# Two units at a time from unit 8 on, in the spectral stage of a Fourier layer with a gated feed-forward part

## The chip, the cores and the metric

One core of one Trainium2 chip. The metric is the time of one execution in microseconds on the device, lower is better. The engines are named as the profile names them: PE (TensorE), DVE (VectorE), ACT (ScalarE), POOL (GpSimd) and SP, whose queue issues every DMA of this kernel.

## The reference

For x of 8 x 3136 x 256, a Fourier transform along the 3136 positions, a complex 256 x 256 mix with bias, a soft threshold at 0.01, the transform back, and then a feed-forward part with a convolution of width 3 and a gate:

```python
X = np.fft.rfft(x, axis=1)
Yr = Xr @ w_r - Xi @ w_i + b_r
Yi = Xr @ w_i + Xi @ w_r + b_i
Yr, Yi = [np.sign(Y) * np.maximum(np.abs(Y) - 0.01, 0) for Y in (Yr, Yi)]
y = np.fft.irfft(Yr + 1j * Yi, n=3136, axis=1)
h = np.maximum(y @ w_in, 0)                      # 1024 channels
out = (h * sigmoid(conv3(h, conv_w))) @ w_out
```

## The kernel before, in words

3136 is 49 x 64, so each transform is two stages of small matrix products with a twiddle table between them. The work of the first 467 us of the span is cut into 50 *units* (`items`, L470): six groups of four frequencies for each of eight batches, and one more unit for each half of the batches. A unit passes through these steps:

- *Stage one* is not per unit but per *piece* (64 pieces of x): four products of 49 x 64 on quarters of the PE array (`quads`, L333), copied out by ACT and DVE (L350, L351), and stored to DRAM by SP. A unit has one or two pieces beside it, as long as pieces last (through unit 40).
- *Stage two* (`stage2`, L384): the rows `a2` come back from DRAM, and eight full-width products fill two PSUM banks, one for each half t of the 256 features. The results must be split into a high and a low part for the mix. For each half ACT copies the imaginary part into d (L387) and casts the whole into fh (L388); DVE makes d, the difference of the two (L389), and fl, the rest that the cast leaves (L390).
- *The third, derived part* (`third`): ACT casts d into fh (L395), and POOL forms its rest in fl (L396).
- *Mix* (`mix`, L412): 36 products of 128 x 256 into three banks c = 2, 0, 1, where c = 2 is the derived part. Each product reads fh or fl as the stationary operand. DVE then adds bank 2 to the bias for both outputs (L415) and joins banks 0 and 1 (L417).
- *Shrink* (`shrink`): two relus on ACT (L428, L429) and their difference on POOL (L430).
- *Stage three* (`stage3_pe`, L440, L443): sixteen products on quarters of the array, into the double bank `psa`, of which there is one; ACT copies it out as z1 (L450) and SP stores it.

PSUM has eight banks: `psa` takes two, and all other products share a ring of six, in the order in which they are asked for.

The order is written out by hand: inside this part each engine takes its instructions in the order of the program. Turn `it` of the loop at L571 issues stage three of unit it-4, the pieces, stage two of unit it, shrink of unit it-2, the third part of unit it, and the mix of unit it-1. So a unit's split is made a whole turn before its mix.

Beside this, `later` (L287) makes the weights of the feed-forward part out of 64-bit numbers, in small DVE *steps*, three a unit from unit 8 to 43. Ten steps (L264 to L271, L279, L280) make one block; the ninth, L279, subtracts what a cast on ACT (L278) leaves, and waits for it. In the last units *stage four* of the first batch (`stage4`, L159) is placed between the others. The feed-forward part after the units (L655 to L701) is not touched.

Of the kernel before, what the change touches and what calls it, by code (L numbers as in the profile page):

```python
# [9 lines left out]
F32 = mybir.dt.float32  # L10
# [13 lines left out]
SP = 64  # L24
H = C // 2
LAM = 0.01
UG = 4
# [84 lines left out]
def spectral_ffn_kernel(ctx: ExitStack, tc: tile.TileContext, x, w_r, w_i, b_r, b_i,  # L112
# [61 lines left out]
    with ExitStack() as ab:  # L174
# [198 lines left out]
                nc.sync.dma_start(a2[0:C], sc0[b // BH].rearrange("b j d -> j b d"))  # L373
            return a2

        def stage2(g, a2):

            fh, fl = [wkf.tile([P, NT, 3, UG, SP], F32R, name=nm) for nm in ("fh", "fl")]
            d = wkf.tile([P, NT, UG, SP], F32, name="d", bufs=DB)
            for t in range(NT):  # L380
                ps = psx.tile([P, UG, 2, SP], F32, name="ps_s2", tag="bank")
                for k in range(UG):
                    kk, q = (K2, g * UG + k) if g < NG else (C, U)
                    nc.tensor.matmul(ps[:, k], a2[0:kk, k, t * P:(t + 1) * P], t2[0:kk, q, :],  # L384
                                     start=(k == 0), stop=(k == UG - 1), skip_group_check=True)
                psv = ps.rearrange("p k c m -> p c k m")
                nc.scalar.copy(d[:, t], psv[:, 1])  # L387
                nc.scalar.copy(fh[:, t, 0:2], psv)  # L388
                nc.vector.tensor_tensor(d[:, t], psv[:, 0], d[:, t], op=ALU.subtract)  # L389
                nc.vector.tensor_tensor(fl[:, t, 0:2], psv, fh[:, t, 0:2].bitcast(F32), op=ALU.subtract)  # L390
            return fh, fl, d

        def third(xs):
# [2 lines left out]
            nc.gpsimd.tensor_tensor(fl[:, :, 2], d, fh[:, :, 2].bitcast(F32), op=ALU.subtract)  # L396
            return fh, fl

        def mix(xs):


            fh, fl = xs
            ps = {c: psx.tile([K2, UG // 2, D], F32, name=f"ps_mx{c}", tag="bank") for c in (2, 0, 1)}
            for c in (2, 0, 1):
                q = (1, 2, 0)[c]
                for k in range(UG // 2):
                    mm = []
                    for t in range(NT):
                        a = [f[:, t, c, 2 * k:2 * k + 2, :] for f in (fh, fl)]
                        mm += [(a[0], wmix_hi[:, t, q, :]), (a[0], wmix_lo[:, t, q, :]), (a[1], wmix_hi[:, t, q, :])]  # L410
                    for n, (lt, rh) in enumerate(mm):
                        nc.tensor.matmul(ps[c][:, k, :], lt, rh, start=(n == 0), stop=(n == len(mm) - 1))  # L412
            v = wk.tile([K2, 2, UG // 2, D], F32, name="v")
            for c in range(2):
                nc.vector.tensor_tensor(v[:, c], ps[2], bias[:, c:c + 1, :].to_broadcast([K2, UG // 2, D]), op=ALU.add)  # L415
            for c in range(2):
                nc.vector.tensor_tensor(v[:, c], ps[c], v[:, c], op=ALU.add)  # L417
            return v

        def clip(v):  # L420
# [9 lines left out]
            nc.gpsimd.tensor_tensor(r, r, v, op=ALU.subtract)  # L430
            return r

        def stage3_pe(g, r):
            ps = psa.tile([P, 2, UG // 2, D], F32, name="ps_s3")
            for a in range(2):
                for k in range(UG // 2):
                    for h in range(2):
                        rows = slice(SP * h, SP * (h + 1))
                        if g < NG:
                            nc.tensor.matmul(ps[SP * a:SP * (a + 1), h, k, :], i1[rows, a, g * UG // 2 + k, :], r[rows, a, k, :],  # L440
                                             start=(k == 0), stop=(k == UG // 2 - 1), skip_group_check=True)
                        else:
                            nc.tensor.matmul(ps[0:SP, h, k, :], i1[rows, a, U // 2, :], r[rows, a, k, :],  # L443
                                             start=(a + k == 0), stop=(a + k == UG // 2), skip_group_check=True)
            return ps

        def stage3_out(b, g, ps):
            z1 = io.tile([P, 2, UG // 2, D], F32, name="z1", bufs=2)
            n = P if g < NG else SP
            nc.scalar.copy(z1[0:n], ps[0:n])  # L450
            if g < NG:
                z1 = z1.rearrange("p h k e -> p (h k) e")
                for c in range(2):
# [18 lines left out]
        LAG, WP0, LATE, NW, NF0, NF1 = 4, 8, 10, 7, 14, 3  # L472
        xs, vs, ss, a2s, xq, pair = {}, {}, {}, {}, {}, []
        p1 = nx = NX

# [8 lines left out]
        def next_s1(p):  # L484
            return stage1_pe(xq[p // 2][:, p % 2])
# [68 lines left out]
        Y0, Y1 = n_it - 6, n_it - 1  # L554
        jgs = iter(range(NPC))

        def one_by_one():
# [10 lines left out]
            stage4(jg, z2, y0, one_by_one)  # L568
            ask_z2()

        for it in range(n_it + LAG):  # L571
            drain = it >= n_it
            if it:
                fetch(1)
            if 2 < it + 2 < NG and it % 2 == 0:
                load_t2(it + 2)
            elif it == LATE:
                load_t2(NG)
                load_inv1(NG)
# [5 lines left out]
            if drain:  # L585
                last_stage()
            if it >= LAG:
                g3 = items[it - LAG]
                ps3 = stage3_pe(g3[1], ss.pop(it - LAG))
            n_s1 = min(2 if 0 < it < 5 else (1, 2, 1, 1, 2, 1)[(it - 5) % 6] if it else 0, n_pc - p1)  # L590
            ps1 = [next_s1(p1 + i) for i in range(n_s1)] if it > 1 else []
            if it >= LAG:
                stage3_out(*g3, ps3)
            if WP0 <= it < Y0:
                next(background, None)
            elif it == WP0 - 2:
                next(background)
            for ps in ps1:
                stage1_out(p1, ps)
                p1 += 1  # L600
            ask_a2(it + 1)
            if WP0 <= it < Y0:
                for _ in range(2):
                    next(background, None)
            if it < n_it:
                xs[it] = stage2(items[it][1], a2s.pop(it))
            if it == Y0:
# [6 lines left out]
            if it == n_it - 1:  # L614
                xs[it] = third(xs[it])
            if 0 <= it - 2 < n_it:
                ss[it - 2] = (clip if drain else shrink)(vs.pop(it - 2))
            if it < n_it - 1:
                xs[it] = third(xs[it])
            if Y0 < it < Y1:  # L620
                last_stage()
            if it == 1:
                for _ in range(n_s1):
                    stage1_out(p1, next_s1(p1))
                    p1 += 1
            if 0 <= it - 3 < NG:
                fill_inv1(it - 3)
            if 0 <= it - 1 < n_it:
                vs[it - 1] = mix(xs.pop(it - 1))
# [121 lines left out]
```

## Time and profile before

| what | value |
|---|---|
| median of 3 runs | 1677.89 us (1676.13 to 1679.12) |
| the profiled execution | 1675.06 us, span 1673.3 us |
| PE busy | 1660.5 us, 99% of the span |
| DVE, ACT, POOL busy | 1388.7, 1177.1, 192.3 us |
| last stage three of the units begins | 465.05 us |
| first product of the feed-forward part | 466.92 us |

The page gives busy times of the engines, the span in 40 slices, the chain of work that ended last, and the costliest groups of instructions. In the timeline a row reads: start in us, length in us, engine, line, operation, tiles written and read, shapes, count, and in brackets the idle time before it with what ended it. A row of waits reads: engine, tile and line that waited, what it waited for, us in total, times, longest. PEld is the loading of a stationary operand, which runs beside the products.

### The profile page before, as it was taken

Reading aid. Unit: us, or ns where it says so; the run is one execution under the profiler, and the core shown is the slowest. Engines: PE = TensorE matmul, PEld = TensorE weight load, DVE = VectorE, ACT = ScalarE, POOL = GpSimd, SP = SyncE. Lnnn points to the kernel's source line nnn. Section 1 sums busy time; section 2 is a strip of 40 time slices with the busy share of each in tenths; the row PEclk is TensorE's granted clock in tenths of the full one; section 3 lists DMA queues with packets and bytes.
Section 4 is the critical chain, followed back from the end, with each engine's and each line's share of the span. In section 5 each row is a group of like instructions: output and inputs, shape, how many; then the busy total and the mean of one; then the engine's idle time right before and its main releaser. Section 6 shows DMA issues by size and latency. Waiting matters only on the chain.

```text
span 1673.3 us, 30664 instructions
## 1 busy us (share of the span) xinstructions
PE 1660.5 (99%) x12618; PEld 1541.2 (92%) x12618; DVE 1388.7 (83%) x1728; ACT 1177.1 (70%) x1585; POOL 192.3 (11%) x114
## 2 busy tenths in 40 slices
PE   9899999999999999999999999999999999999998
PEld 5788888889999999999999999999999999999998
DVE  3578888877688888888888888888888888888887
ACT  3577777777677677777677776767777776776776
POOL 1444444445300000000000000000000000000000
PEclk9999999999999999999999999999999999999999
DMA  8999999886421111111110111111101111100001
GB/s 228 282 292 291 259 268 270 248 230 190 109 81 42 51 33 42 52 52 42 52 47 27 42 36 36 43 52 52 33 33 52 52 34 50 42 23 23 23 23 45
DMA packets 108297, 162.29 MB, mean 97 GB/s; under 512 B 10842, under 2 KB 87806, under 8 KB 108094
## 3 DMA queue, kind: packets, MB, share of 16 engines
q1 hardware_dynamic: 108158, 160.34, 32.4%
q8 instruction: 100, 1.64, 0.4%
q14 instruction: 39, 0.32, 0.1%
HBM read 83.24 MB, written 77.07 MB: 96 GB/s over the span
## 4 chain that ended last, share of the span: by engine, by line
PE 98%; DMA 1%; issue 0%; SPq 0%; ACT 0%; ACTq 0%
PE acc L690 33%; PE ps_h L655 33%; PE ps_mx L412 13%; PE ps_s L159 7%; PE ps_s L384 6%; PE ps_s L333 3%; PE ps_s L440 3%; DMA a<-sch 0%; DMA hx<-in_x_dram 0%; PE ps_idle L509 0%; PE ps_s L443 0%; DMA sch<-ha 0%; SPq L316 0%; ACT o L696 0%; SPq L347 0%
## 5 line engine op out<-in xcount | busy, mean ns | idle before, releaser
L690 PE MATMUL acc<-wout,gh 128*128 128x256 f32 x3136 | 567.4, 281 | 0.4 <-ACT gh L676 0.4
L671 DVE SCALAR_TENSOR_TENSOR c<-h,cw,c 128x896 f32<-128x896 f32 x448 | 513.2, 1147 | 65.0 <-ACT c L669 63.8
L655 PE MATMUL ps_h<-yh,win 128*128 128x450 f32 (+1 forms) x1792 | 546.5, 366 | 0.0
L690 PEld LDWEIGHTS acc<-wout,gh 128*128 128x128 f32 x3136 | 491.0, 188 | 6.1 <-ACT gh L676 0.6
L690 PE MATMUL acc<-wout,gl 128*128 128x256 f32 x1568 | 436.0, 280 | 0.0
L665 ACT ACTIVATE h<-ps_h 128x898 f32<-128x898 f32 (+1 forms) x224 | 207.2, 925 | 231.6 <-PE ps_h L655 231.4
L655 PEld LDWEIGHTS ps_h<-yh,win 128*128 128x128 f32 x1792 | 337.6, 188 | 26.0 <-issue 0.4
L655 PE MATMUL ps_h<-yl,win 128*128 128x450 f32 (+1 forms) x896 | 328.7, 367 | 0.0
L690 PEld LDWEIGHTS acc<-wout,gl 128*128 128x128 f32 x1568 | 293.1, 188 | 0.2
L673 DVE TENSOR_TENSOR c<-h,c 128x896 f32<-128x896 f32 x224 | 243.6, 1088 | 48.1 <-ACT c L672 47.0
L677 DVE TENSOR_TENSOR gl<-c,gh 128x896 fp32r<-128x896 f32 x224 | 243.2, 1088 | 35.4 <-ACT gh L676 31.4
L676 ACT CAST gh<-c 128x896 fp32r<-128x896 f32 x224 | 210.5, 945 | 81.2 <-DVE c L673 81.1
L672 ACT ACTIVATE c<-c 128x896 f32<-128x896 f32 x224 | 213.5, 953 | 23.8 <-DVE c L671 21.1
L655 PEld LDWEIGHTS ps_h<-yl,win 128*128 128x128 f32 x896 | 168.5, 188 | 10.1
L669 ACT ACTIVATE c<-h,cw 128x896 f32<-128x896 f32 x168 | 175.5, 1045 | 2.9 <-DVE gl L677 0.2
L412 PE MATMUL ps_mx<-wmix_hi,fh 128*128 128x256 f32 x600 | 172.2, 287 | 0.0
L412 PE MATMUL ps_mx<-wmix_lo,fh 128*128 128x256 f32 x600 | 167.6, 279 | 0.0
L412 PE MATMUL ps_mx<-wmix_hi,fl 128*128 128x256 f32 x600 | 167.1, 279 | 0.0
L430 POOL TENSOR_TENSOR r<-r,v 128x1024 f32<-128x1024 f32 x48 | 114.5, 2385 | 217.8 <-ACT v L429 200.2
L384 PEld LDWEIGHTS ps_s<-t,a 128*128 128x128 f32 (+1 forms) x800 | 94.7, 194 | 37.9 <-issue 23.0
L159 PEld LDWEIGHTS ps_s<-i,z 98*128 98x128 f32 x1024 | 122.5, 192 | 1.9 <-issue 0.8
L159 PE MATMUL ps_s<-i,z 98*128 98x98 f32 x1024 | 123.3, 273 | 0.0
(93 smaller groups left out, 1672.7 us busy)
## 6 DMA issues: line engine op xcount, KB each, us to landing
z<-sc SPq DMA_DIRECT2D x64, 392.0 KB
sc<-z SPq DMA_DIRECT2D x96, 256.0 KB
out_dram<-o SPq DMA_DIRECT2D x27, 896.0 KB
xr<-in_x_dram SPq DMA_DIRECT2D x112, 192.0 KB
sc<-a SPq DMA_DIRECT2D x56, 384.0 KB
a<-sc SPq DMA_DIRECT2D x42, 512.0 KB
hx<-in_x_dram SPq DMA_DIRECT2D x16, 192.0 KB
a<-sch SPq DMA_DIRECT2D x6, 512.0 KB
```

The costliest lines, as they stand in the source:

```text
L159: nc.tensor.matmul(to, z2[:, j, t * P:(t + 1) * P], i2[:, 0 if jg or j else 1, :], start=(j == 0), stop=(j == JG - 1), skip_group_check=True)
L384: nc.tensor.matmul(ps[:, k], a2[0:kk, k, t * P:(t + 1) * P], t2[0:kk, q, :], start=(k == 0), stop=(k == UG - 1), skip_group_check=True)
L412: nc.tensor.matmul(ps[c][:, k, :], lt, rh, start=(n == 0), stop=(n == len(mm) - 1))
L655: nc.tensor.matmul(dst, lt, rh, start=(i == 0), stop=(i == len(mm) - 1))
L665: nc.scalar.activation(hv, src, AF.Relu)
L669: nc.scalar.mul(cv, tap(0), cw[:, 0, f:f + 1])
L671: nc.vector.scalar_tensor_tensor(cv, tap(k), cw[:, k, f:f + 1], cv, op0=ALU.mult, op1=ALU.add)
L672: nc.scalar.activation(c, c, AF.Sigmoid)
L673: nc.vector.tensor_tensor(cv, tap(1), cv, op=ALU.mult)
L676: nc.scalar.copy(gh, c)
L677: nc.vector.tensor_tensor(gl, c, gh.bitcast(F32), op=ALU.subtract)
L690: nc.tensor.matmul(acc[m // 2][:, m % 2, :], lt[:, sl], rh[:, f, :], start=(f == 0 and n == 0 and m % 2 == 0), stop=(f == NF - 1 and n == ...
```

## The change

Units 0 to 7 keep their turns. From unit 8 on a turn takes two units, u and u+1. On PE it issues stage three of u-4, up to two pieces, stage three of u-3, the other pieces; then both second stages; then both mixes. Where no piece lies between the two stage threes, the second takes two banks of the ring and not `psa`. In a pair:

- the mix of u follows the second stages of u and u+1 directly. In before it followed the next unit's second stage, pieces and stage three;
- DVE makes d for both halves and then fl for both halves, where it made d, fl, d, fl;
- the mix takes the derived part last: banks 0, 1, 2, and the bias is added to banks 0 and 1, bank 2 joined after;
- the relus of u-1 and u stand after both second stages, around the mix of u;
- of six steps a pair, four stand around the pieces, one before the mix of u and one after the relus of u;
- x is asked for at the start of the turn and again behind the pieces; a2 of u+2 at the start and behind the pieces, a2 of u+3 behind the second stage of u.

The core of the diff:

```diff
-        def stage2(g, a2):
+        def stage2(g, a2, paired=False):
+            made = []
...
                 nc.scalar.copy(d[:, t], psv[:, 1])
                 nc.scalar.copy(fh[:, t, 0:2], psv)
-                nc.vector.tensor_tensor(d[:, t], psv[:, 0], d[:, t], op=ALU.subtract)
-                nc.vector.tensor_tensor(fl[:, t, 0:2], psv, fh[:, t, 0:2].bitcast(F32), op=ALU.subtract)
+                made.append((t, psv))
+                if t or not paired:
+                    for k, src in made:
+                        nc.vector.tensor_tensor(d[:, k], src[:, 0], d[:, k], op=ALU.subtract)
+                    for k, src in made:
+                        nc.vector.tensor_tensor(fl[:, k, 0:2], src, fh[:, k, 0:2].bitcast(F32), op=ALU.subtract)
+                    made = []
...
-        def mix(xs):
+        def mix(xs, paired=False):
...
-            for c in (2, 0, 1):
+            order = (0, 1, 2) if paired else (2, 0, 1)
+            for c in order:
...
+        for u in range(PAIR, n_it, 2):
+            busy = u < Y0
+            ask_a2(u + 2)
+            fetch(2)
...
+            z = s3(u - LAG)
+            out1 = pieces(min(n_s1, 2))
+            next(out1)
+            if busy:
+                steps(2)
+            stage3_out(*z)
+            next(out1, None)
+            if busy:
+                steps(1)
+            z = s3(u + 1 - LAG, not n_s1)
+            out1 = pieces(max(n_s1 - 2, 0))
+            next(out1)
+            stage3_out(*z)
+            next(out1, None)
+            if busy:
+                steps(1)
+            fetch(2)
+            ask_a2(u + 2)
...
+            for i in (u, u + 1):
+                xs[i] = third(stage2(items[i][1], a2s.pop(i), True))
+                if i == u:
+                    ask_a2(u + 3)
+                if u > Y0:
+                    last_stage()
...
+            ss[u - 1] = shrink(vs.pop(u - 1))
+            if busy:
+                steps(1)
+            vs[u] = mix(xs.pop(u), True)
+            ss[u] = shrink(vs.pop(u))
+            if busy:
+                steps(1)
+            vs[u + 1] = mix(xs.pop(u + 1), True)
+
+        for n in range(2):
+            z = s3(n_it - LAG + n)
+            last_stage()
+            stage3_out(*z)
+            if n == 0:
+                ss[n_it - 1] = clip(vs.pop(n_it - 1))
+            last_stage()
+        z = [s3(n_it - 2 + n, n) for n in range(2)]
+        for q in z:
+            stage3_out(*q)
```

On PE, in the turn of unit 12 before: stage three, two pieces, one second stage, and the mix of unit 11 (fh_1594, while the second stage at hand belongs to unit 12).

```order
L440 MATMUL ps_s3_1667<-r_1503,i1_465 64x256 x8
L333 MATMUL ps_s1_1676<-xr_1226,f1_118 64x512 x2
L333 MATMUL ps_s1_1677<-xr_1226,f1_118 64x512 x2
L333 MATMUL ps_s1_1682<-xr_1446,f1_118 64x512 x2
L333 MATMUL ps_s1_1683<-xr_1446,f1_118 64x512 x2
L384 MATMUL ps_s2_1706<-t2_122,a2_1559 128x128 x4
L384 MATMUL ps_s2_1715<-t2_122,a2_1559 128x128 x4
L412 MATMUL ps_mx2_1730<-wmix_hi_125,fh_1594 128x256
L412 MATMUL ps_mx2_1730<-wmix_lo_126,fh_1594 128x256
L412 MATMUL ps_mx2_1730<-wmix_hi_125,fl_1595 128x256
```

The same unit now, in the pair of units 12 and 13, from the pair's second stage three on: fh_1788 and fl_1789 are the split of ps_s2_1791 and ps_s2_1798, four rows above.

```order
L463 MATMUL ps_s3_1751<-r_1609,i1_465 64x256 x8
L333 MATMUL ps_s1_1760<-xr_1300,f1_118 64x512 x2
L333 MATMUL ps_s1_1761<-xr_1300,f1_118 64x512 x2
L385 MATMUL ps_s2_1791<-t2_122,a2_1559 128x128 x4
L385 MATMUL ps_s2_1798<-t2_122,a2_1559 128x128 x4
L385 MATMUL ps_s2_1816<-t2_122,a2_1584 128x128 x4
L385 MATMUL ps_s2_1823<-t2_122,a2_1584 128x128 x4
L419 MATMUL ps_mx0_1841<-wmix_hi_125,fh_1788 128x256
L419 MATMUL ps_mx0_1841<-wmix_lo_126,fh_1788 128x256
L419 MATMUL ps_mx0_1841<-wmix_hi_125,fl_1789 128x256
```

The mix has moved next to its own unit's second stage, with one other second stage between them; the third product reads fl.

On DVE before, one unit's split and the adds behind the mix (d and fl in turn for the two halves):

```order
L389 TENSOR_TENSOR d_2033<-ps_s2_2034,d_2033 128x256
L390 TENSOR_TENSOR fl_2032<-ps_s2_2034,fh_2031 128x512
L389 TENSOR_TENSOR d_2033<-ps_s2_2043,d_2033 128x256
L390 TENSOR_TENSOR fl_2032<-ps_s2_2043,fh_2031 128x512
L415 TENSOR_TENSOR v_2097<-ps_mx2_2058,bias_123 128x512 x2
L417 TENSOR_TENSOR v_2097<-ps_mx0_2059,v_2097 128x512
L417 TENSOR_TENSOR v_2097<-ps_mx1_2060,v_2097 128x512
```

And now, in the pair of units 18 and 19: the splits of both units, a step, then the adds of the first mix.

```order
L393 TENSOR_TENSOR d_2446<-ps_s2_2447,d_2446 128x256
L393 TENSOR_TENSOR d_2446<-ps_s2_2454,d_2446 128x256
L395 TENSOR_TENSOR fl_2445<-ps_s2_2447,fh_2444 128x512
L395 TENSOR_TENSOR fl_2445<-ps_s2_2454,fh_2444 128x512
L393 TENSOR_TENSOR d_2471<-ps_s2_2472,d_2471 128x256
L393 TENSOR_TENSOR d_2471<-ps_s2_2479,d_2471 128x256
L395 TENSOR_TENSOR fl_2470<-ps_s2_2472,fh_2469 128x512
L395 TENSOR_TENSOR fl_2470<-ps_s2_2479,fh_2469 128x512
L268 TENSOR_SCALAR win_m_2389<-win_bits_1972 128x512
L423 TENSOR_TENSOR v_2536<-ps_mx0_2497,bias_123 128x512
L423 TENSOR_TENSOR v_2536<-ps_mx1_2498,bias_123 128x512
```

The first fl now stands behind the second d.

On ACT now, in the pair of units 16 and 17: the third casts, the relus of unit 15 (v_2151), a weight cast, the relus of unit 16, and the copy of the next stage three.

```order
L401 CAST fh_2239<-d_2241 128x2x256
L447 ACTIVATE r_2262<-v_2151,small_86 128x1024
L448 ACTIVATE v_2151<-v_2151,small_86 128x1024
L278 CAST win_0_82<-win_m_1977 128x512
L447 ACTIVATE r_2312<-v_2307,small_86 128x1024
L448 ACTIVATE v_2307<-v_2307,small_86 128x1024
L477 COPY z1_2394<-ps_s3_2363 128x1024
```

Before, a cast of this kind stood between the copies:

```order
L450 COPY z1_1903<-ps_s3_1888 128x1024
L278 CAST win_0_82<-win_m_1589 128x512
L350 COPY a1_1909<-ps_s1_1897 128x2x256
L387 COPY d_1924<-ps_s2_1925 128x256
L388 CAST fh_1922<-ps_s2_1925 128x512
```

It has moved from the head of a unit's copies to a place behind two relus.

More of the change, by code (lines that the diff above doesn't have):

```diff
@@ L397, in third @@
             return fh, fl
-        def mix(xs):
+        def mix(xs, paired=False):
             fh, fl = xs
-            ps = {c: psx.tile([K2, UG // 2, D], F32, name=f"ps_mx{c}", tag="bank") for c in (2, 0, 1)}
-            for c in (2, 0, 1):
+            order = (0, 1, 2) if paired else (2, 0, 1)
+            ps = {c: psx.tile([K2, UG // 2, D], F32, name=f"ps_mx{c}", tag="bank") for c in order}
+            for c in order:
                 q = (1, 2, 0)[c]
@@ L413, in mix, with biased, joined @@
             v = wk.tile([K2, 2, UG // 2, D], F32, name="v")
[L414 to L417, printed above, removed]
+            def biased(c, src):
+                nc.vector.tensor_tensor(v[:, c], ps[src], bias[:, c:c + 1, :].to_broadcast([K2, UG // 2, D]), op=ALU.add)
+            def joined(c, src):
+                nc.vector.tensor_tensor(v[:, c], ps[src], v[:, c], op=ALU.add)
+            if paired:
+                for c in range(2):
+                    biased(c, c)
+                for c in range(2):
+                    joined(c, 2)
+            else:
+                for c in range(2):
+                    biased(c, 2)
+                for c in range(2):
+                    joined(c, c)
             return v
@@ L431, in shrink, with stage3_pe @@
             return r
-        def stage3_pe(g, r):
-            ps = psa.tile([P, 2, UG // 2, D], F32, name="ps_s3")
+        def stage3_pe(g, r, ring=False):
+            if ring:
+                ps = [psx.tile([P, UG // 2, D], F32, name="ps_s3", tag="bank") for _ in range(2)]
+            else:
+                both = psa.tile([P, 2, UG // 2, D], F32, name="ps_s3")
+                ps = [both[:, h] for h in range(2)]
             for a in range(2):
@@ L449, in stage3_out @@
             n = P if g < NG else SP
-            nc.scalar.copy(z1[0:n], ps[0:n])
+            if isinstance(ps, list):
+                for h in range(2):
+                    nc.scalar.copy(z1[0:n, h], ps[h][0:n])
+            else:
+                nc.scalar.copy(z1[0:n], ps[0:n])
             if g < NG:
@@ L553, in spectral_ffn_kernel @@
         background = later()
-        Y0, Y1 = n_it - 6, n_it - 1
+        Y0 = n_it - 6
         jgs = iter(range(NPC))
@@ L569, in last_stage, with steps, s3, pieces @@
             ask_z2()
-        for it in range(n_it + LAG):
-            drain = it >= n_it
+        def steps(n):
+            for _ in range(n):
+                next(background, None)
+        def s3(i, ring=False):
+            b, g = items[i]
+            return b, g, stage3_pe(g, ss.pop(i), ring)
+        def pieces(n):
+            nonlocal p1
+            todo = [next_s1(p1 + i) for i in range(n)]
+            yield
+            for ps in todo:
+                stage1_out(p1, ps)
+                p1 += 1
+        for it in range(PAIR):
             if it:
@@ L598, in spectral_ffn_kernel @@
-            for ps in ps1:
-                stage1_out(p1, ps)
-                p1 += 1
-            ask_a2(it + 1)
[L602 to L607, printed above, removed]
+                z = s3(it - LAG)
+            n_s1 = 2 if 0 < it < 5 else (1, 2, 1, 1, 2, 1)[(it - 5) % 6] if it else 0
+            if it > 1:
+                out1 = pieces(n_s1)
+                next(out1)
@@ L613, in spectral_ffn_kernel @@
                     ask_z2()
[L614 to L629, printed above, removed]
+            ss[u - 1] = shrink(vs.pop(u - 1))
[4 more added lines that the diff above has]
+            if busy:
+                steps(1)
+            vs[u + 1] = mix(xs.pop(u + 1), True)
+        for n in range(2):
+            z = s3(n_it - LAG + n)
+            last_stage()
+            stage3_out(*z)
+            if n == 0:
[4 more added lines that the diff above has]
+            stage3_out(*q)
         assert p1 == n_pc and not z2s and next(background, True)
```

48 lines of the change are left out of this document (30 added, 18 removed).

## The prediction, made before the changed kernel was run

> **What bounds the kernel now.** I read the page first, then the list of waits, the stretches, and the timeline of one unit. The page's busy times and its chain of waits:
>
> ```profile
> PE 1660.5 (99%) x12618; PEld 1541.2 (92%) x12618; DVE 1388.7 (83%) x1728; ACT 1177.1 (70%) x1585; POOL 192.3 (11%) x114
> PE 98%; DMA 1%; issue 0%; SPq 0%; ACT 0%; ACTq 0%
> ```
>
> The chain is TensorE almost from end to end. Its waits, longest and last, and one stretch of the unit stage:
>
> ```profile
> PE ps_s L333 <- issue: 5.0, 1, 5.0
> ...
> PE acc L690 <- ACT gh L676: 0.4, 1, 0.4
> ```
>
> ```profile
> 200.00:250.00 50.00, 50.00 (x471) 41.96 (x470) 43.44 (x74) 37.02 (x58) 22.88 (x12) 1.00 0.97 266
> ```
>
> The 5.0 us lie at 43 us, before the units that change. From there on TensorE waits for nobody, at clock 1.00, while VectorE works 43.44 of 50 us and ScalarE 37.02. So nothing is to be gained but TensorE's own handovers, and any wait that the new order brings is lost whole. The timeline of a unit with one piece, and the start of the next, which has two:
>
> ```profile
> 200.31 0.28 PE L412 MATMUL ps_mx<-wmix_lo,fh 128*128 128x256 f32 x1
> 200.43 0.27 PE L412 MATMUL ps_mx<-wmix_hi,fl 128*128 128x256 f32 x1
> 200.64 1.11 PE L440 MATMUL ps_s<-r,i 64*64 64x256 f32 x16
> 201.55 1.05 PE L333 MATMUL ps_s<-xr,f 49*64 49x512 f32 x8
> 201.83 1.01 ACT L450 COPY z<-ps_s 128x1024 f32<-128x1024 f32 x1 [1.68 <-PE ps_s L440]
> 202.53 2.05 PE L384 MATMUL ps_s<-t,a 128*128 128x128 f32 x16
> 204.05 0.59 ACT L388 CAST fh<-ps_s 128x512 fp32r<-128x512 f32 x1
> 204.34 0.37 PE L412 MATMUL ps_mx<-wmix_hi,fh 128*128 128x256 f32 x1
> 204.55 0.19 PEld L412 LDWEIGHTS ps_mx<-wmix_hi,fl 128*128 128x128 f32 x1
> 204.73 0.42 DVE L389 TENSOR_TENSOR d<-ps_s,d 128x256 f32<-128x256 f32 x1
> 204.89 0.59 ACT L388 CAST fh<-ps_s 128x512 fp32r<-128x512 f32 x1
> 204.90 0.19 PEld L412 LDWEIGHTS ps_mx<-wmix_hi,fl 128*128 128x128 f32 x1
> 205.07 0.68 DVE L390 TENSOR_TENSOR fl<-ps_s,fh 128x512 fp32r<-128x512 f32 x1
> 205.67 0.41 DVE L389 TENSOR_TENSOR d<-ps_s,d 128x256 f32<-128x256 f32 x1
> 208.76 1.11 PE L440 MATMUL ps_s<-r,i 64*64 64x256 f32 x16
> 209.68 1.91 PE L333 MATMUL ps_s<-xr,f 49*64 49x512 f32 x16
> 211.52 2.05 PE L384 MATMUL ps_s<-t,a 128*128 128x128 f32 x16
> ```
>
> Each group begins where the one before it hands over: 0.91 us stage three, 0.98 one piece (1.84 two), 1.81 second stage, 4.42 mix. In this order the mix at 204.34 reads the unit before, whose splits are long done. The unit whose second stage began at 202.53 is mixed a whole unit later. That distance is what the change gives up.
>
> **What the change saves.** *Mix to stage three.* Mix matmuls follow each other at 0.12 us (200.31, 200.43); the next stage three comes 0.21 after the last. So 0.09 is lost once a unit, now once a pair: 21 x 0.09 = 1.9 us. Both ends are nearly equal, since second stage to mix shows no such loss.
>
> *Pieces to second stage.* A second piece costs 1.84 - 0.98 = 0.86, so the handover from a piece to the second stage is 0.12. It is now paid once a pair. The new handover, piece to stage three, is in no trace. Another row:
>
> ```profile
> 377.62 1.11 PE L440 MATMUL ps_s<-r,i 64*64 64x256 f32 x16
> 378.66 2.05 PE L384 MATMUL ps_s<-t,a 128*128 128x128 f32 x16
> ```
>
> Stage three straight into the second stage takes 1.04 where stage three into a piece takes 0.91: full-width loads behind quarter tiles pay 0.13. Between quarter tiles it can cost nothing or up to the same 0.12. I take half: 21 x 0.06 = 1.3 us, ends 0 and 2.5. A loss beyond that is excluded, since no handover in the rows is dearer than 0.13.
>
> *The end.* The last stage-four group is followed by one stage three, then by the first matmul of the next part:
>
> ```profile
> 465.05 1.94 PE L443 MATMUL ps_s<-r,i 64*64 64x256 f32 x16
> 466.92 0.19 PEld L655 LDWEIGHTS ps_h<-yh,win 128*128 128x128 f32 x1 [0.39 <-issue]
> ```
>
> These 1.87 hold 1.04 of work and 0.83 of waiting for y. In the new order two stage threes stand there and cover it: 0.8, ends 0 and 0.8. Saved in all 4.0 us, between 1.9 and 5.2.
>
> **What it costs: the splits come too late.** Put the start of second stage u at 0. A second stage with other full-width matmuls behind it takes 1.89:
>
> ```profile
> 407.64 2.05 PE L384 MATMUL ps_s<-t,a 128*128 128x128 f32 x16
> 409.53 1.93 PE L159 MATMUL ps_s<-i,z 98*128 98x98 f32 x16
> ```
>
> So mix u would begin at 1.89 + 1.81 = 3.70. It loads fl of the first half 0.21 later (204.55 - 204.34) and of the second half 0.56 later (204.90): wanted at 3.91 and 4.26. The other side: the cast fh of the second half ends at 204.89 + 0.59 - 202.53 = 2.95. VectorE starts 0.09 after such a cast (204.64 to 204.73), and now does both d first: the second d starts at 3.04, the first fl 0.34 later (204.73 to 205.07) at 3.38, the second 0.60 after that (205.07 to 205.67) at 3.98. With 0.68 each they end at 4.06 and 4.66; with the same 0.09 to wake TensorE, 4.15 and 4.75. TensorE waits 0.24 at its third mix matmul and 0.25 more at its sixth: **0.49 a pair**. The old order d, fl, d, fl (first d at 2.11 + 0.09) would start the second fl at 3.48 and end it at 4.16, just in time: both d first is what moves it. In pairs 46 and 48 a stage-four group stands between and covers the wait. The other 19 pairs pay: 19 x 0.49 = 9.3 us. If the wake cost nothing it would be 19 x 0.40 = 7.6; if ScalarE or VectorE were 0.3 late, 15.
>
> Mix u+1 is safe: its splits have 4.3 us more. The derived part goes through GpSimd:
>
> ```profile
> L396 POOL TENSOR_TENSOR fl<-d,fh 128x512 fp32r<-128x512 f32 x31 | 46.9, 1513 | 0.0
> ```
>
> Its cast can start at 3.55, ends near 4.2, and 1.51 more gives 5.8; with the derived part last it is wanted only 24 matmuls (2.8 us) into the mix, at 7.0. Cover 1.2 us. Without it, first in the mix, TensorE would wait until 5.8, two more us a pair.
>
> *A cast in ScalarE's row.* Six weight steps go with each pair and ten make one weight block, so in pairs 16 and 26 the step ahead of mix u's bias adds is the subtraction L279, which needs the cast L278. That cast now stands behind both relus of unit u-1. Rows of the waits and of the relus:
>
> ```profile
> DVE wout_m L279 <- ACT wout L278: 4.3, 3, 2.0
> ```
>
> ```profile
> 205.37 1.17 ACT L428 ACTIVATE r<-v,small 128x1024 f32<-128x1024 f32 x1
> ...
> 206.57 1.16 ACT L429 ACTIVATE v<-v,small 128x1024 f32<-128x1024 f32 x1
> ```
>
> Today that wait is up to 2.0 us too, and idle time of VectorE hides it. In the pair, bias adds, joins, the relus of unit u and the copy of the next stage three queue behind it. The copy ordinarily ends 201.83 + 1.01 - 200.64 = 2.2 after stage three begins, and the pair's second stage three wants that bank at 0.91 + 1.72 = 2.63. Relus of 2.3 us behind a block of some 2.5 leave the copy 1 to 3 us late. I take 2 for each of the two pairs: 4 us, ends 0 and 6. In pair 40, with one piece, the bank is wanted at 0.91 + 0.86 = 1.77, so 0.5 more.
>
> *At no cost.* The asks on SP's queue: a row that loads next is asked a pair ahead, over 16 us, where the old order asked at
>
> ```profile
> 205.17 0.38 SPq L371 DMA_DIRECT2D a<-sc x1
> ```
>
> for a second stage two units on, 14 us, and TensorE never waited for one. SP's waits on the copies z1 stand ahead of the asks for x, but x is held three buffers ahead, more than a pair. If that cover went, a late load would show as second stages waiting on DMA.
>
> **The sum.** 9.3 + 4 + 0.5 - 4.0 = +9.8 us. The profiled execution is 1675.06 us (span 1673.3 and 1.8 around it), so 1684.9 by its own clock. The median of the runs shown is 1677.89, 2.8 above it; on that the forecast is **1687.7 us**. A measurement here can tell about 0.2%, 3.4 us, from no change.
>
> **Rivals.** *No wait (faster).* If fl came 0.5 us sooner than worked out, only the savings stay, with the 0.5 of pair 40: 1677.89 - 3.5 = 1674.4. It decides at the sixth mix matmul: second fl in by 4.26. For it: only 0.49 has to be found, and the chain is eight rows long. Against it: every row of it repeats over hundreds of instructions. Chance 0.10.
>
> *Half of it (no change).* If a wait is partly the handover that I count as saved, say 0.25 a pair, and the cast is hidden as it is today: 4.8 + 0.5 - 4.0, 1679.2. Chance 0.17.
>
> *VectorE becomes the bound (slower still).* It has the least room: from stage three's start, joins end at 1.4, two steps, two piece copies, step, copy, step fill it to about 6.0, and d is wanted at 4.55 + 2.2 = 6.8. The steps read and write the on-chip memory that GpSimd's adds use:
>
> ```profile
> 216.78 2.38 POOL L430 TENSOR_TENSOR r<-r,v 128x1024 f32<-128x1024 f32 x1 [4.91 <-ACT v L429]
> 218.41 1.03 DVE L266 TENSOR_SCALAR wout_e<-wout_e 128x512 int32<-128x512 int32 x1
> ...
> 212.28 0.42 DVE L264 TENSOR_SCALAR wout_e<-wout_bits 128x512 int32<-128x512 int32 x1
> ```
>
> The same kind of step takes 0.42 alone and 1.03 under the add, ending 0.28 after the add does. The pair now puts both adds r, 2.38 each, after the splits, so a step can fall under a whole one: up to 2.3 lost, of which 0.8 is slack, 1.5 at worst. With half, 0.7, in the 11 pairs of three pieces: 7.7 more, 1695.4. The Trainium skill, "SBUF — State Buffer", section "Who interferes with whom", says that of such a pair the one issued second blocks until the first has finished; by that rule the whole add counts, the trace agrees (the step ended only after the add), and the worst case would be 11 x 1.5 = 16.5 us. Against it: today's steps meet the same adds and VectorE has 6 of 50 us idle. Chance 0.11.
>
> **Chances.** Forecast 0.62, no wait 0.10, half 0.17, VectorE 0.11. The forecast's own bounds are 7.6 + 0 - 5.2 = +2.4 and 15 + 6 + 0.5 - 1.9 = +19.6; I cut the upper one, since all its ends together are unlikely. Range 1677.5 to 1694.0: it leaves out the no-wait case and most of the VectorE case. Faster by over 0.2%: 0.10. Within: 0.20 (half, and the low end of the forecast). Slower: 0.70.
>
> **What would show it.** Right: in the waits of the new profile mix matmuls wait for VectorE's fl, some 0.25 us twice in a pair and 19 times, at the third and sixth matmul; two pairs near weight casts show stage three waiting for ScalarE's z1; the mix-to-stage-three gap of 0.21 comes once in two units. Wrong: TensorE still without waits in the unit stage; or waits on DMA, or on bias adds in most pairs, which would be the VectorE case.

## The result and the profile after

| | before | changed |
|---|---|---|
| median, us | 1677.01 (1675.93 to 1679.12, 4 runs) | 1700.15 (1697.18 to 1702.54, 4 runs) |
| ratio | | 1.0135, 95% interval 1.0119 to 1.0152 |
| span of the profiled execution, us | 1673.3 | 1696.2 |

The change costs 23 us. The sign was forecast; the size was not, and 1700.15 lies above the range. A pair is named below by its first unit: pair 20 is the turn of units 20 and 21.

The page of the changed kernel, busy times and chain of waits:

```profile
PE 1665.7 (98%) x12618; PEld 1549.6 (91%) x12618; DVE 1410.7 (83%) x1726; ACT 1183.3 (70%) x1592; POOL 190.5 (11%) x115
PE 91%; DMA 4%; DVE 1%; ACT 1%; issue 1%; SPq 1%; ACTq 0%; DVEq 0%
```

Of the chain, 98% was TensorE; it is 91% now, and DMA, which had 1%, has 4%. Its list of waits on TensorE:

```profile
PE ps_s L385 <- DMA a<-sc: 7.8, 4, 2.3
...
PE ps_s L463 <- ACT z L477: 2.6, 3, 1.1
PE ps_s L333 <- DVE a L351: 1.9, 2, 1.0
```

Four second stages (L385) wait for a2, up to 2.3 us each. Before, TensorE waited for no a2 from unit 8 on. Two third pieces (L333) are late by 1.0 each. The list puts that down to VectorE's copy a, but in pair 20 the last load of the piece's x tile lands in the same tenth of a microsecond (216.17, the copy ends at 216.23, the piece starts at 216.30); e15 below shows that it is x. The same 50 us as in the prediction:

```profile
200.00:250.00 50.00, 46.62 (x431) 40.54 (x434) 44.77 (x71) 35.22 (x54) 20.72 (x12) 1.00 0.93 249
```

TensorE now works 46.62 of 50 us, where it worked all 50. Neither VectorE nor ScalarE is full.

**The forecast wait, as forecast.** The start of a mix, pair 10, in the timeline:

```profile
130.33 1.27 DVE L395 TENSOR_TENSOR fl<-ps_s,fh 128x512 fp32r<-128x512 f32 x2
130.44 0.36 PE L419 MATMUL ps_mx<-wmix_hi,fh 128*128 128x256 f32 x1
130.65 0.28 PE L419 MATMUL ps_mx<-wmix_lo,fh 128*128 128x256 f32 x1
131.06 0.19 PEld L419 LDWEIGHTS ps_mx<-wmix_hi,fl 128*128 128x128 f32 x1 [0.34 <-DVE fl L395]
...
131.65 0.19 PEld L419 LDWEIGHTS ps_mx<-wmix_hi,fl 128*128 128x128 f32 x1 [0.18 <-DVE fl L395]
```

The third and the sixth product wait, together 0.5 us. Most pairs' 72 mix matmuls take 9.08 us from first start to the next group; in pairs 46 and 48, which have a stage-four group in between, they take 8.58.

**The wait that was not forecast.** SP's row between the pieces of pair 18 and those of pair 20, and TensorE's row in pair 20 (L338 and L342 store a1, L316 and L319 load x, L371 loads a2):

```profile
204.49 1.36 SPq L338 DMA_DIRECT2D sc<-a  x2
205.89 2.10 SPq L342 DMA_DIRECT2D sc<-a  x1
208.09 3.10 SPq L316 DMA_DIRECT2D xr<-in_x_dram  x4
211.24 0.54 SPq L319 DMA_DIRECT2D xr<-in_x_dram  x1
211.88 1.79 SPq L316 DMA_DIRECT2D xr<-in_x_dram  x4
213.79 0.51 SPq L319 DMA_DIRECT2D xr<-in_x_dram  x1
214.80 1.27 SPq L371 DMA_DIRECT2D a<-sc  x2
```

```profile
214.23 1.09 PE L463 MATMUL ps_s<-r,i 64*64 64x256 f32 x16
216.30 1.20 PE L333 MATMUL ps_s<-xr,f 49*64 49x512 f32 x8 [0.98 <-DVE a L351]
217.43 2.05 PE L385 MATMUL ps_s<-t,a 128*128 128x128 f32 x16
221.67 2.02 PE L385 MATMUL ps_s<-t,a 128*128 128x128 f32 x16 [2.19 <-DMA a<-sc]
```

The a2 row of unit 21 is asked, in the program, right behind the second stage of unit 18, near 200.5 by the trace. SP issues it only at 214.80: stores and ten x loads stand ahead. TensorE wants it at 217.43 + 1.81 = 219.24 and goes on at 221.67, 6.9 us after the issue. The third piece, at 216.30 instead of 215.1, is late as well. Pairs 14, 20, 26 and 32 have such waits. In each of them three pieces follow a pair that also had three, and in that pair two x tiles came free at once.

**The cast.** Pair 16's mix and the stage threes of pair 18:

```profile
187.81 0.60 ACT L278 CAST win<-win_m 128x512 fp32r<-128x512 f32 x1
187.98 2.40 POOL L449 TENSOR_TENSOR r<-r,v 128x1024 f32<-128x1024 f32 x1 [0.93 <-ACT v L448]
188.44 2.48 DVE L279 TENSOR_TENSOR win_m<-win_m,win 128x512 f32<-128x512 f32 x1 [2.30 <-ACT win L278]
190.85 1.27 DVE L423 TENSOR_TENSOR v<-ps_mx,bias 128x512 f32<-128x512 f32 x2
...
193.35 1.15 ACT L447 ACTIVATE r<-v,small 128x1024 f32<-128x1024 f32 x1 [4.95 <-DVE v L426]
...
196.79 1.11 PE L463 MATMUL ps_s<-r,i 64*64 64x256 f32 x16 [1.14 <-ACT z L477]
```

Cast behind relus, subtraction behind cast, bias adds behind subtraction, relus behind those, and the copy z1 last. The subtraction L279 also falls under GpSimd's add and takes 2.48 us; alone, at 128.34, it takes 0.68. The stretch from pieces to the second stage three takes 4.29 us in place of 1.72; after pair 26 it is 3.01. Both together are 3.9 too long.

**The end.** The last stage three and the first products of the feed-forward part:

```profile
485.52 1.89 PE L466 MATMUL ps_s<-r,i 64*64 64x256 f32 x16
...
487.34 0.47 PE L738 MATMUL ps_h<-yh,win 128*128 128x448 f32 x1
...
489.51 1.06 ACT L475 COPY z<-ps_s 64x512 f32<-64x512 f32 x2 [2.66 <-DMA sc<-z]
...
490.62 0.47 PE L738 MATMUL ps_h<-yh,win 128*128 128x448 f32 x1 [0.58 <-ACT z L475]
```

The last copies z1 wait 2.66 us until a z1 buffer is stored, and `ps_h` waits for the banks that they empty. The first 60 matmuls of that part take 14.19 us, 12.30 before. Ahead of them TensorE waits for nothing:

```profile
484.00:488.00 4.00, 4.00 (x42) 2.81 (x41) 1.41 (x7) 2.38 (x6) 0.00 (x0) 1.00 0.95 283
```

The last unit's stage three (L466, in before L443) is simply longer than the others. Its sixteen products all write partitions 0 to 63, where those of other units write both halves, and in the trace they start two at a time, 0.21 us apart, where the others start four at a time. VectorE has made the last of y by 486.10. In before the last of these products starts at 466.61, the feed-forward part at 466.92.

**A pair without transfer waits.** TensorE's row in pair 16 up to the next turn:

```profile
175.25 1.11 PE L463 MATMUL ps_s<-r,i 64*64 64x256 f32 x16
176.17 1.91 PE L333 MATMUL ps_s<-xr,f 49*64 49x512 f32 x16
177.89 1.09 PE L463 MATMUL ps_s<-r,i 64*64 64x256 f32 x16
178.91 3.84 PE L385 MATMUL ps_s<-t,a 128*128 128x128 f32 x32
191.58 0.68 PE L463 MATMUL ps_s<-r,i 64*64 64x256 f32 x8
```

16.33 us, of which 0.50 is the wait for fl: 15.83 of work, where two units of one piece each took 16.21 (192.55 to 208.76 before). TensorE saves 0.38 in this pair and 0.34 in pair 46 (17.68, where two units with a stage-four group each took 18.02), over twice the 0.15 that the prediction took.

### The profile page after: what moved, and what is told of

It reads as the page before. It is cut to its first block, busy times and chain, and to the rows that moved or that the text cites. A ratio compares the mean times of both kernels' runs of the same rounds, so it can differ in the third digit from the quotient of the medians.

```text
span 1696.2 us, 30708 instructions
## 1 busy us (share of the span) xinstructions
PE 1665.7 (98%) x12618; PEld 1549.6 (91%) x12618; DVE 1410.7 (83%) x1726; ACT 1183.3 (70%) x1592; POOL 190.5 (11%) x115
## 4 chain that ended last, share of the span: by engine, by line
PE 91%; DMA 4%; DVE 1%; ACT 1%; issue 1%; SPq 1%; ACTq 0%; DVEq 0%
PE acc L773 32%; PE ps_h L738 32%; PE ps_mx L419 11%; PE ps_s L159 6%; PE ps_s L385 5%; PE ps_s L333 2%; PE ps_s L463 2%; DMA a<-sc 2%; DMA xr<-in_x_dram 1%; SPq L316 1%; DMA sc<-z 0%; DMA hx<-in_x_dram 0%; PE ps_idle L536 0%; ACT z L477 0%; DMA a<-sch 0%
## 5 line engine op out<-in xcount | busy, mean ns | idle before, releaser
L755 ACT ACTIVATE c<-c 128x896 f32<-128x896 f32 x224 | 213.5, 953 | 25.7 <-DVE c L754 22.9
L419 PE MATMUL ps_mx<-wmix_hi,fl 128*128 128x256 f32 x600 | 171.1, 285 | 0.9 <-DVE fl L395 0.8
L385 PEld LDWEIGHTS ps_s<-t,a 128*128 128x128 f32 (+1 forms) x800 | 94.2, 195 | 29.2 <-issue 16.2
```

The costliest lines, as they stand in the source:

```text
L755: nc.scalar.activation(c, c, AF.Sigmoid)
```

## The experiments

The theory after the result: half of the loss is the forecast one (fl, cast), the other half is SP's row (an a2 that stands behind x loads). The rivals: the transfers are simply too many, in any order; or one loss hides another. Ratios are to the kernel before, with 95% intervals. Most rows have four runs, and those of one edit lie up to 8 us apart (e2: 1692.27 to 1700.18), so two edits less than some 3 us apart are not told from each other; e12 has two runs, e11, e14 and e15 have 11 or 12.

| edit to the changed kernel | median, us | ratio |
|---|---|---|
| none | 1700.15 | 1.0135 (1.0119 to 1.0152) |
| e1: both x tiles behind a2 | 1706.69 | 1.0171 (1.0154 to 1.0188) |
| e2: d, fl, d, fl | 1697.17 | 1.0120 (1.0101 to 1.0139) |
| e3: step ahead of the relus | 1693.99 | 1.0100 (1.0081 to 1.0120) |
| e5: e1 + e2 + e3 | 1698.73 | 1.0129 (1.0114 to 1.0144) |
| e6: no later weight words | 1698.87 | 1.0135 (1.0113 to 1.0157) |
| e7: e2 + e3 | 1689.91 | 1.0082 (1.0066 to 1.0098) |
| e8: e7 + e6 | 1689.46 | 1.0079 (1.0058 to 1.0101) |
| e9: e7, a2 asked by ScalarE | 1756.78 | 1.0475 (1.0460 to 1.0491) |
| e10: one x tile, a2, the other | 1692.56 | 1.0092 (1.0077 to 1.0106) |
| e11: e7 + e10 | 1678.93 | 1.0015 (1.0005 to 1.0024) |
| e12: derived part first | 1709.65 | 1.0191 (1.0173 to 1.0208) |
| e13: e7, x asked once a turn | 1709.60 | 1.0187 (1.0172 to 1.0201) |
| e14: e11, end as before | 1676.14 | 0.9994 (0.9985 to 1.0003) |
| e15: e14, first x tile earlier | 1672.89 | 0.9982 (0.9972 to 0.9991) |

**e1, a2 ahead of x.**

```diff
-            fetch(2)
             ask_a2(u + 2)
...
                 if i == u:
                     ask_a2(u + 3)
+                    fetch(2)
```

> Edit: the second ask for x of a turn is moved behind the ask for the a2 row of unit u+3, nothing else. Theory A (order on SP's queue): second stages of turns 14, 20, 26, 32 waited 1.6 to 3.0 us each for an a2 row that stood behind ten x loads; asked ahead of them it lands in time, 9.3 us less, 1691; if the third pieces of turns 20 and 26 (1.2 each) waited for an x that is now earlier or later by the same queue, 1688 to 1693. Theory B (the transfers themselves are too many in those turns, whatever their order): the wait moves to the pieces or to other turns and the time stays within 3 us of 1700.

Slower by 6.5 us, which neither theory gave. The second stages no longer wait for a2 (0.4 us in all); the third pieces wait for x, in pair 20 and in three more:

```profile
222.74 2.10 PE L333 MATMUL ps_s<-xr,f 49*64 49x512 f32 x8 [4.53 <-DMA xr<-in_x_dram]
```

The eight matmuls of a piece, 1.09 at other places, took 2.10 here. The stretches of that trace say why; the last column but two is TensorE's granted clock:

```profile
220.00:222.00 2.00, 0.00 (x0) 0.00 (x0) 0.30 (x1) 0.00 (x0) 0.00 (x0) 0.90 0.98 205
222.00:224.00 2.00, 1.26 (x8) 0.45 (x8) 0.00 (x0) 0.00 (x0) 0.00 (x0) 0.50 0.85 187
224.00:226.00 2.00, 2.00 (x10) 1.24 (x7) 1.13 (x2) 0.58 (x1) 0.00 (x0) 0.50 1.10 370
```

After the wait the clock is 0.50, and the second stages behind the piece take 5.32 us in place of 3.59. Here the wait was paid a second time in the work behind it. What this run leaves open is whether the transfers are too many, or whether this order is only wrong the other way.

**e2, d and fl by half.**

```diff
-                xs[i] = third(stage2(items[i][1], a2s.pop(i), True))
+                xs[i] = third(stage2(items[i][1], a2s.pop(i)))
```

> Edit: in the pairs VectorE does d, fl, d, fl again instead of d, d, fl, fl. Theory A (the distance lost is 0.5 us and the order of the four operations makes it): the second fl ends some 0.6 us earlier and the first a whole 1.3 us earlier, both just in time, so the 0.50 us in each of 19 mixes goes: 9.7 us less, 1690.5, at least 7 less if the second still comes 0.1 late. Theory B (the distance itself is too short, in any order): the third matmul stops waiting, the sixth waits longer by what the third no longer does; the time stays within 2 us of 1700.

In the trace, pair 10 again, the first fl is done before the mix begins and the sixth product follows in turn:

```profile
130.98 0.36 PE L419 MATMUL ps_mx<-wmix_hi,fh 128*128 128x256 f32 x1
...
131.30 0.28 PE L419 MATMUL ps_mx<-wmix_hi,fl 128*128 128x256 f32 x1
...
131.65 0.38 PE L419 MATMUL ps_mx<-wmix_hi,fl 128*128 128x256 f32 x1
```

The 72 matmuls take 8.57 to 8.75 in 17 of 19 pairs, and 7.2 of the 9.7 us went; it is the order of the four operations that made the wait, not the distance. Yet the median fell by only 3, which four runs do not tell from nothing. The two second stages of pairs 14, 20 and 26 take 7.28, 6.12 and 6.49 us, where the changed kernel has 5.22, 6.02 and 5.82 and 3.60 is the time without a wait; the pieces behind the cast in pair 18 take 5.04 in place of 4.29. So 3.5 of the 7.2 us came back as longer waits, most of them for a2.

**e3, the step ahead of the relus.**

```diff
-            ss[u - 1] = shrink(vs.pop(u - 1))
             if busy:
                 steps(1)
+            ss[u - 1] = shrink(vs.pop(u - 1))
             vs[u] = mix(xs.pop(u), True)
```

> Edit: the weight step ahead of the mix of unit u is issued before the relus of unit u-1, nothing else. Theory A (in pairs 16 and 26 the cast stands behind both relus on ScalarE, the subtraction that needs it holds the bias adds on VectorE, and the copy z1 comes late): the stage threes of turns 18 and 28 stop waiting, 4.7 us less, 1695.5. Theory B (VectorE is full there and the subtraction costs the same wherever it stands): under 1.5 us less.

6 us less. Pairs 18 and 28 are back at 1.72, and the subtraction L279 is no longer under GpSimd's add, only under its shorter operation that makes fl, and takes 1.45 us in place of 2.48. Theory A holds; 4.7 and 6 are not told apart by four runs (1688.92 to 1696.98).

**e5, all three.** The diffs of e1, e2 and e3 together.

> Edits of the three other runs of this set together. If the three losses are apart from each other they add: 1700 - 9.3 - 9.7 - 4.7 = 1676.3, with the two pieces another 2.4 less, 1673.9: equal to or up to 3 us below the kernel before (1677). If one loss only hides another, less than the sum goes: 1682 or above.

1698.73, so the losses did not add, and it is the second case. There are 16.1 us of waits on x in five pairs, where e1 has 12.4 in four. On top of e1 the other two edits take 8.0 us off; the loss that e1 brings eats nearly all of it.

**e6, fewer bytes.** The later weight blocks read the words of the first two again, so six of the eight 512 KB loads of these words, and the right weights of the feed-forward part, are left out.

```diff
-                asked.append((dst, load_bits(src, WP, nm), WP, nm))
+                if n < 2:
+                    kept.append(load_bits(src, WP, nm))
+                asked.append((dst, kept[n % 2], WP, nm))
```

> Edit: of the weight blocks only the first two are read from DRAM; every later block takes the words of one of these two again, so the weights of the feed-forward part are other numbers and all instructions but some thirty 512 KB loads stay. Theory C (transfers at their limit: SP's row never idle, DMA share 0.9 to 1.0, so what is late is only a question of what stands last): each turn of 16.5 us has 0.6 of such a load less, about 0.75 us of transfer time; the row catches up and the waits of second stages for a2 (9.3 us) and of third pieces (2.4 us) go for the most part: 1688 to 1692. Theory A (the order of asks alone): the ten x loads still stand ahead of a2, the waits stay, 1698 to 1701.

The expectation speaks of some thirty loads; the trace of the changed kernel has eight, this one two. Nothing changed: the second stages of pairs 14, 20, 26 and 32 are 9.4 us too long, where the changed kernel's are 9.3, and the ratio is the same. **e7** has e2 and e3 together, **e8** e7 and the edit of e6.

> The edits of the runs on d, fl by half and on the cast ahead of the relus, together, with a2 asked where the change asks it. If losses add, 9.7 in the mixes and 4.7 to 6 at the cast go: 1685. Theory C: what TensorE saves makes it arrive earlier at transfers that come no sooner, so most of the 9.7 turns up again as waits of second stages for a2: 1690 to 1695.

> The same two edits, and the weight words left out as in the first run of this set (other weights, same instructions). Theory C: with transfer time to spare both gains show, the a2 waits are under 3 us in all: 1674 to 1679, at the kernel before or below. Theory A: the a2 waits stay at 9 us or more: 1684 or above.

1689.91 and 1689.46. So 10 us of the two gains show and some 5 do not. e7 ends at the edge of what theory C gave, and part of the gain did turn up again as waits: the same second stages are 13.0 us too long. But the lighter kernel of e8, which by theory C should have come to 1679 or less, gained nothing. This is no strong test: six loads are 3 of the 87 MB moved between 90 and 470 us, and no weight load stands in SP's row between the pieces of pair 18 and those of pair 20; the next comes behind, at 227.7. Whether the sum of the transfers is the limit is settled by e10.

**e9, a2 on ScalarE's queue.** On top of e7, in the pairs:

```diff
-                nc.sync.dma_start(a2, ...)
+                nc.scalar.dma_start(a2, ...)
```

> The same two edits, weights whole again, and in the pairs a2 is asked on ScalarE's queue and no longer behind the x loads on SP's. Theory A: a2 then lands without waiting for the ten x loads, and x is where the change has it: 1676 to 1679. Theory C: the same sixteen DMA engines carry both; a2 comes in time and x, z or the pieces are late in its place, 8 us or more of waits on x: 1686 to 1695.

Neither: 1756.78. The timeline of ScalarE shows why this run tells nothing of the two:

```profile
166.82 0.37 ACTq L372 DMA_DIRECT2D a<-sc  x1
167.28 0.37 ACT L389 COPY d<-ps_s 128x256 f32<-128x256 f32 x1 [7.26 <-DMA sc<-a]
```

The a2 load has to come behind stores of a1, which are on the other queue now; ScalarE stands still until they have landed (56.4 us in ten such waits), and the splits with it.

**e10, one x tile, then a2, then the other.** Left to try was the order by need. Of the two tiles the first is wanted by the third piece of the next turn, the second a turn later.

```diff
-            fetch(2)
+            fetch(1)
             ask_a2(u + 2)
...
                 if i == u:
                     ask_a2(u + 3)
+                    fetch(1)
```

> Edit to the changed kernel: of the second ask for x only one tile is asked ahead of the two a2 rows, the other behind the a2 of unit u+3. Theory D (bunching: SP's row stands still until the copies z1 of a turn, then carries five groups of stores and, where a turn frees two x tiles, ten x loads ahead of a2; the first of the two tiles is wanted by the third piece of the next turn, the second only a turn later): a2 is asked 2.5 us earlier and x no later than it is wanted, so the waits of the second stages (9.4 us) go and the pieces of turns 20 and 26 keep at most their 2.4: 1700 - 9.4 = 1690.5, 1688 to 1692. Rival (what is moved from a2 comes back on x, as when both x tiles stood behind a2): waits on x of 5 us or more, 1697 or above.

1692.56, half a microsecond above theory D's range and 4 below the rival's. SP's row at the same place, then TensorE's in pair 20:

```profile
206.74 3.05 SPq L316 DMA_DIRECT2D xr<-in_x_dram  x4
209.84 0.54 SPq L319 DMA_DIRECT2D xr<-in_x_dram  x1
210.48 0.39 SPq L371 DMA_DIRECT2D a<-sc  x1
210.91 1.89 SPq L316 DMA_DIRECT2D xr<-in_x_dram  x4
```

```profile
215.11 1.09 PE L333 MATMUL ps_s<-xr,f 49*64 49x512 f32 x8
216.13 3.84 PE L385 MATMUL ps_s<-t,a 128*128 128x128 f32 x32
```

a2 is issued 4.3 us earlier; both second stages run through, here and in pairs 14, 26 and 32. The third pieces of pairs 26 and 32 are 0.9 us late, where those of pairs 20 and 26 were 1.2 late. The same 50 us as above:

```profile
200.00:250.00 50.00, 50.00 (x468) 42.60 (x468) 46.85 (x72) 37.73 (x58) 22.13 (x12) 1.00 0.96 255
```

TensorE works all of them, at a DMA share of 0.96 where the changed kernel had 0.93. No bytes were taken away, and no row was moved but the second x tile. So the transfers fit, and theory C falls.

**e11, the same with e2 and e3.**

> The same edit on top of d, fl by half and the cast ahead of the relus. Theory D: the second stages of five turns were 13 us longer there, and the mixes behind them 4 us more at a lower clock; most of both goes: 1690 - 15 = 1675, 1673 to 1678, at the kernel before (1676.5) or up to 3 us below. Rival (the gain in TensorE's own work is given back at the transfers whatever stands first): 1684 or above.

1678.93, one above theory D's range: 11 us less than e7 by this one edit, which alone took 7.6. Singly the three edits take 3.0, 6.2 and 7.6 us, 16.7 in all; together they take 21.2. While one cause stood it hid part of the others' cures.

**e12, the derived part first.**

```diff
-            order = (0, 1, 2) if paired else (2, 0, 1)
+            order = (2, 0, 1)
...
-            if paired:
+            if False:
```

> Edit to the changed kernel: the derived part stands first in the mix of the pairs again (with the bias added to it), nothing else. Theory: the third part of fl comes from GpSimd 1.5 us after its cast, at about 5.8 us from the start of second stage u, and the mix wants it at 3.9: 2 us a pair in place of 0.5, so 19 x 1.5 = 28 us more, 1728; with the clock lowered by the waits up to 1740. Rival (the wait is covered by something else, so that where the derived part stands does not matter): 1697 to 1704.

9.5 us slower, not 28. In pair 10 of its trace:

```profile
129.96 0.38 PE L419 MATMUL ps_mx<-wmix_hi,fh 128*128 128x256 f32 x1 [0.27 <-ACT fh L401]
...
131.38 0.38 PE L419 MATMUL ps_mx<-wmix_hi,fl 128*128 128x256 f32 x1 [0.92 <-POOL fl L402]
```

Second stages and mixes together take 13.9 us in most pairs, 12.7 in the changed kernel: 1.2 a pair where 1.5 was expected, some 22 in 18 pairs. Part of it came back: the waits for a2 are 4.8 in all in place of 7.8, the third pieces' are all but gone, that behind the cast in pair 18 is 1.3 in place of 2.6, together 6.7. The start-up (units 0 to 7) of this execution is 2.3 shorter besides; the rest of the way from 22 to 9.5 was not traced. Here a slower TensorE waited less for transfers.

**e13, x asked once a turn**, on top of e7:

```diff
-            fetch(2)
             ask_a2(u + 2)
```

> On top of d, fl by half and the cast ahead of the relus, x is no longer asked behind the pieces, only at the head of the next turn. Theory D: a2 stands ahead of every x tile, but the tile that the third piece of the next turn wants is asked only at that turn's head, behind nothing but with some 4 us to go: a wait of several us for x wherever three pieces follow three, 10 us or more in all, 1695 or above. Theory A (what is wrong is only x ahead of a2): 1676 to 1680.

As theory D had it, 1709.60, with 22.5 us of waits on x in five pairs. The second ask for x is needed; only its second tile had the wrong place.

**e14 and e15, what was still open.** e14 puts the end back: a stage-four group ahead of each of the last four stage threes, all in `psa`. e15 also moves the first x tile of a turn ahead of the second pair of stores:

```diff
+            fetch(1)
             z = s3(u + 1 - LAG, not n_s1)
...
-            fetch(1)
             ask_a2(u + 2)
```

> On top of the three edits of the run that came to 1678.9 (half, cast, one x tile ahead of a2), the tail is ordered as in the kernel before: a stage-four group ahead of each of the last four stage threes, all in the same bank, one stage three left for the end. Theory: the last two stage threes side by side covered nothing (2.74 us for two where 1.87 for one, with y no earlier) and left the copies z1 and the ring's banks to hold the first products of the feed-forward part: its first group of 60 matmuls goes from 14.96 back to 12.3, the tail is 0.4 longer; 2.3 us less, 1676.6. Rival (the first group is late for another reason, such as ScalarE's h): 14.9 stays, 1679.3.

> The same, and the first x tile of a turn is asked behind the first two pieces and ahead of the second pair of stores, no longer behind all pieces. Theory D (the third piece of turns 14, 20, 26 and 38 waits 0.3 to 1.9 us each for a tile that stands behind the turn's second stores): these 4 us go, 1672.5, below the kernel before (1677) by 3 to 5 us. Rival (in turns where one tile is freed only by the last piece nothing is asked earlier, and what is asked earlier pushes the stores, z1 copies and a2 back): 1675 to 1680.

1676.14 and 1672.89. In both, the first 60 matmuls of the feed-forward part take 12.30 us again. In e15 the third piece follows the stage three by 0.86 to 0.87 us in every pair that has one, where e14 has up to 1.99 (pair 26); only an ask for x was moved between the two, so the late third pieces were waiting for x. This version is the fastest here, 0.18% (0.09 to 0.28) below the kernel before. Its page:

```profile
PE 1653.6 (99%) x12618; PEld 1546.8 (92%) x12618; DVE 1387.3 (83%) x1726; ACT 1183.6 (71%) x1591; POOL 190.6 (11%) x115
```

One a2 in pair 16 was still 3.6 us late in this profiled execution, which took 1675.87, 3 us over the median; the reason was not looked for.

## Why the prediction was right in part and wrong in size

*Splits too late, 0.49 a pair, 9.3 us:* right. 0.50 in a plain pair, at the two products named, and made by "both d first" (e2). Over the 19 pairs the mixes are 9.7 us too long. That the total comes so near is partly luck: pairs 14, 20 and 26 pay next to none of it, since the wait for a2 covers it, and pairs 18, 28 and 32 pay 0.7 to 1.1 each, behind the cast or at a lower clock.

*The cast, 2 for each of two pairs, and 0.5 in pair 40:* right. 2.6 and 1.3; 0.6. e3 shows the cause.

*The asks on SP's queue, no cost:* this step failed, and its own sign came true ("a late load would show as second stages waiting on DMA"). It took the place of the ask in the program for the time at which SP gets to it. a2 is asked over 16 us ahead, but SP issues it 14 us later, since its row now carries the stores of two units in one piece and, where two x tiles come free together, ten x loads ahead of a2. That x is three tiles ahead did not help: it is what filled the row. Measured: 9.3 us in second stages and 2.4 in pieces. e10 shows it to be the order and not the bytes: with the same bytes the waits for a2 are gone.

*The end, 0.8 saved:* this failed too. The 1.87 us were read as 1.04 of work and 0.83 of waiting for y, by the stage three of the other units; but the last unit's takes that long in itself, so there was no wait to cover, and the two together took 2.74. Besides, the ring banks and the two z1 buffers made the first 60 products 1.9 late, and the rest of the feed-forward part took 0.6 longer, which was not followed up. In place of 0.8 saved, 2.5 were lost; e14 gives the 1.9 back.

*Savings of 1.9 and 1.3:* the direction was right, the size too small: 0.34 to 0.38 a pair in place of 0.15. The gap of 0.21 from mix to stage three does come once in two units (191.37 to 191.58), and the handover from the pieces came out at the favourable end, near 0.12. The rest, about 0.1 a pair in the mixes, has no cause shown here.

*VectorE as the bound:* did not come. A step can fall under a whole add, as the rival said (L264 takes 2.24 us at 196.24, where it took 0.42 before), but in pairs 12, 30, 36 and 38, which have three pieces and no late transfer, TensorE waits for fl alone.

The sum, in the profiled executions: 9.7 for the splits, 3.9 and 0.6 for the cast, 9.3 and 2.4 for the late transfers, 2.5 at the end make 28.4. The unchanged units before 8 took 1.7 longer, which makes 30.1; unit 7's second stage begins between 93.3 and 96.7 us in the runs here (93.89 before, 95.58 in the changed kernel), so that is not laid to the change. The spans differ by 22.9; so 7.2 were saved, 0.34 a pair over 21 pairs, which fits the pairs measured above. Against the forecast of 9.8, 11.7 are the transfers, 3.3 the end and 1.7 the start; savings 4.0 larger than forecast hid part of that.

## What to carry to other kernels

An ask in the program is not an issue: when work is bunched, go along the queue's row in the trace, put down what stands ahead of each load, and order the loads by when each is wanted, tile by tile. Where a transfer is nearly late, savings in the engine and savings in the queue do not show in full singly (16.7 us against 21.2 here); take all the causes away together before you call one of them worthless. Here the shorter work of one engine paid only once the queue's order had followed it. And before a time is called waiting, compare it with the same line's own work at another place, not with that of a neighbour that looks alike.

## What was not expected of the hardware

The granted clock can fall around a wait of TensorE and stay low for some microseconds of work: 0.50 from about 221.6 to 228.4 around the 4.53 us in e1. In the changed kernel a wait of 2.28 us, in pair 32, was followed by a fall:

```profile
330.00:332.00 2.00, 0.76 (x7) 0.79 (x8) 1.51 (x3) 0.62 (x1) 0.89 (x1) 1.00 1.08 357
332.00:334.00 2.00, 2.00 (x14) 2.00 (x13) 0.43 (x1) 0.94 (x3) 0.38 (x1) 0.61 1.04 421
334.00:336.00 2.00, 2.00 (x12) 2.00 (x12) 1.18 (x3) 1.51 (x4) 0.00 (x0) 0.53 1.02 406
```

The wait of 2.19 us in pair 20 cost no clock: 6.02 us for its second stages is 3.60 and the late start. The length of one wait does not decide it: in e2 a wait of 2.50 us, in pair 32, cost no clock either, while in e10 the clock was 0.50 from 195.2 to 198.6 around a wait of 1.14 us, the longest near it. The Trainium skill, "TensorE: Matmul & The Clock Gate", section "What's actually happening", has the clock fall to half after an idle window of about 3.4 us. The half agrees with the 0.50; the length does not agree with the waits of 2.28 and 1.14 us, and the measurement decides.

The DMA share of the stretches, 0.93 in the changed kernel and 0.97 before, did not tell whether transfers were the limit: with one x tile moved (e10) the share was 0.96, and the time 7.6 us less.
